# An order planner that counts two engines' SBUF operations longer in one passage

## The chip, the cores and the metric

The kernel runs on one core of a Trainium2 chip. The metric is the device time of one launch in microseconds (us). Three runs of the kernel before took 804.41, 806.04 and 806.45 us; their median is 806.04.

Six queues matter here: TensorE (PE, matmuls, results in PSUM banks), its weight loads (PEld), VectorE (DVE), ScalarE (ACT), GpSimd (POOL, which here works on SBUF only) and SyncE (SP), which issues DMAs. Each engine takes its instructions strictly in the order in which the program lists them, and waits at the first one whose inputs or destination are not ready.

## The reference

Three stages in a row. Attention over 32 memory slots, for 4 batches of 8 heads and 576 positions, gives a matrix of 2304 tokens by 512. A gated layer of 1536 hidden columns follows, and then a GELU layer of 2048:

```python
x = attn_out.transpose(0, 2, 1, 3).reshape(B * S, H * D)      # 2304 x 512
x = ((x @ moe_w_a) * (x @ moe_w_b)) @ moe_w_out               # 1536 hidden columns
h = x @ moe2_w_in                                             # 2048 hidden columns
out = (h * (1.0 / (1.0 + np.exp(-1.702 * h)))) @ moe2_w_out
```

## The kernel before

**Numbers.** Each float32 operand of a large product is split into a high part (a ScalarE copy that rounds, line 282) and a low part (the difference, line 276). A product then takes three matmul passes: high by high, low by high, high by low.

**First layer.** The 1536 hidden columns go in six groups `g` of 256. For each batch `b` and half `u` of 288 tokens, `gated(g, b, u)` runs 24 matmuls into four PSUM banks (line 800). `gated_out` then copies one bank (ScalarE, line 813), multiplies it by the other (VectorE, line 816) and splits the result into high and low. `proj(g, b, u)` runs 24 matmuls into four banks (line 833), and `proj_out` adds each bank to the sum in `acc` (VectorE, line 887).

**Second layer.** The product with `moe2_w_in` is done by `quad(g, p)`, for a group `g` of 256 hidden columns and a third `p` of the tokens (768 of them). It uses seven products of sums of half blocks in place of eight plain ones. Each product is a `step` of six matmuls of 384 columns (line 1066) into one bank. The first bank is copied (`kept`, ScalarE, line 1101), the other six are added to running sums (`added`, VectorE, line 1108, seven operations for a quad), and `gate` applies GELU and stores the block to DRAM (lines 1118 and 1120). The last stage, `proj2` (line 1174), reads these blocks back.

**The passage between the layers.** Before `quad(g, p)` can run, `combine_tokens(p, r)` (with `r` 0 and 1) must turn the sums in `acc` into seven operands, `yc[p]`, each split in two. By `seven` that is four additions or subtractions and seven splits for each `r`: 22 line-276 operations of 384 columns for one `p`, each on VectorE or on GpSimd, and 14 ScalarE copies. The operand with number 2 comes first, those with numbers 4 and 6 at the end of the chain. The products of a quad use the operands in the order 2, 4, 5, 3, 0, 6, 1. The passage begins when `room_early` is called, within the last group of the first layer. From there the main stream issues to TensorE, in this order: two `proj`, `gated(5,2,0)`, `gated(5,2,1)`, three `proj`, `gated(5,3,0)`, `gated(5,3,1)`, `quad(0,0)`, two `proj`, and then the quads (1,0), (0,1), (1,1), (0,2), (1,2), (2,0) and so on. The operands of `p` = 2 are only placed in `room_projected`, after the last `proj`.

**Buffers.** From the passage on, eight PSUM banks are shared by these steps (`bank_m`). A bank is free again when the last operation that reads it is done. The running sums of the quads (`hb_s`) and a buffer for decoding weights (`dm_s`) lie in the parts of `acc` that are free when `yc[0]` is done.

**Weights.** The float64 weights arrive as pairs of words and are decoded by `decode_piece`, five operations of 512 columns for a piece: ScalarE line 390, a maximum on VectorE or GpSimd (line 392), VectorE lines 396, 400 and 405. Then the raw buffer is free and SyncE can load the next piece into it (line 308).

**What sets the order.** The program is written by a planner, `Order`, when it is built. Each piece of work is a stream that asks for an engine with a ready time and a cost in ns (`dve(n)`, `act(n)`, `pool(n)`). `run` keeps a clock for each engine, and issues at each turn the request that can start first (in steps of 40 ns), among equals the one of lower priority number. PSUM work of `gated_out`, `proj_out`, `kept` and `added` has priority 0, the token operands have 5, 6 and 7. Where a request names two engines, `_plan` takes the one with the smaller sum of start, backlog, cost and `handicap`. The handicap of VectorE is 1000 ns (`W1`) from the end of attention on. The model's clocks decide the order on every engine; they don't wait for anything on the chip. As there is one main stream, the order of TensorE's matmuls in the passage is that of the list above, whatever the costs.

Of the kernel before, what the change touches and what calls it, by code (L numbers as in the profile page):

```python
# [12 lines left out]
ALU = mybir.AluOpType  # L13
# [6 lines left out]
PE, ACT, DVE, POOL = "PE", "ACT", "DVE", "POOL"  # L20
HOP, HOP_PE = 130.0, 200.0
W0 = 300.0
W1 = 1000.0
HOLD = {}
PR = 30
MBN = 8
# [17 lines left out]
def dve(n, fast=False):  # L44
    return 68 + n / (1.92 if fast else 0.96)


def act(n, psum=False):
    return (52 if psum else 94) + n / 1.2


def pool(n):
    return 150 + 2.1 * n


class Slots:


    def __init__(self, tiles=()):
        self.free = [[t, 0.0] for t in tiles]  # L60
# [11 lines left out]
class Order:  # L72
# [9 lines left out]
    def __init__(self):  # L82
        self.clock = {PE: 0.0, ACT: 0.0, DVE: 0.0, POOL: 0.0}
        self.dma, self.marks, self.streams, self.count = 2000.0, {}, [], 0

        self.handicap = {DVE: W0}

    def mark(self, t, *key):
        self.marks[key] = t
# [62 lines left out]
def tile_mem_attention_moe_moe2(  # L152
# [48 lines left out]
    od = Order()  # L201
# [70 lines left out]

    def combine(t, dst, in0, in1, op, n):

        t, e = yield {DVE: dve(n)} if op == ALU.max else {POOL: pool(n), DVE: dve(n)}, t
        (nc.gpsimd if e == POOL else nc.vector).tensor_tensor(out=dst, in0=in0, in1=in1, op=op)  # L276
        return t

    def hi_lo(t, hi, lo, src, n):

        t, _ = yield ACT, t, act(n)
        nc.scalar.activation(out=hi, in_=src, func=AF.Copy)  # L282
        return (yield from combine(t, lo, src, f32(hi), ALU.subtract, n))
# [10 lines left out]
    def raw_of(i):  # L294
        return raw_x if i == 2 * NHG - 1 else raw_s
# [82 lines left out]
    def decode_piece(t, i, name, part, n, m):  # L378

        plain = name[:2] == ("wab", 0)  # L380
        if plain:
            wt[name] = yield "slot", wab0_s
            t = max(t, wt[name][1])
        raw = loaded.pop(("raw", i))
        lw, hw = (raw[0][:, :, j].rearrange("p (n f) -> p n f", n=n) for j in range(2))
        mf = m[0].rearrange("p (n f) -> p n f", n=n)
        mu = mf.bitcast(U32)

        t, _ = yield ACT, t, act(512)
        nc.scalar.activation(out=mf, in_=hw.bitcast(F32), func=AF.Abs)  # L390
        t, e = yield {DVE: dve(512, True), POOL: 1456}, t
        (nc.vector if e == DVE else nc.gpsimd).tensor_scalar(  # L392
            out=mf, in0=mf, scalar1=2.0 ** -15, scalar2=None, op0=ALU.max
        )
        t, _ = yield DVE, t, dve(512, True)
        nc.vector.tensor_scalar(
            out=mu, in0=mu, scalar1=0x07FFFFFF, scalar2=3, op0=ALU.bitwise_and, op1=ALU.logical_shift_left
        )
        t, _ = yield DVE, t, dve(512)
        nc.vector.scalar_tensor_tensor(  # L400
            out=mu, in0=hw, scalar=0xC0000000, in1=mu, op0=ALU.bitwise_and, op1=ALU.bitwise_or
        )
        t, _ = yield DVE, t, dve(512)
        dst = wt[name][0].rearrange("p (n f) -> p n f", n=n) if plain else mf
        nc.vector.scalar_tensor_tensor(
            out=dst.bitcast(U32), in0=lw, scalar=29, in1=mu, op0=ALU.logical_shift_right, op1=ALU.bitwise_or
        )
        raw_of(i).release(raw, t)
        if plain:
            dm_s.release(m, t)  # L410
            od.mark(t, *name, part)
        elif name[0] == "in":
            decoded[name, part] = m
            od.mark(t, "decoded", name, part)
            if part == 1:
                od.spawn(PW if name[1] else PW0, combine_weights(name[1]))
        elif name[0] == "o2":
            c = name[1]
            t = max(t, (yield "mark", "room", *name))
            t = yield from hi_lo(t, wo2[c][:, HI], wo2[c][:, LO], m[0], DM)  # L420
            dm_s.release(m, t)
            od.mark(t, "wo2", c)
        else:
            if part == 0:
                wt[name] = yield "slot", slots_of[name[0]]
                od.mark(wt[name][1], "place", name)
            t = max(t, (yield "mark", "place", name))
            yield from split_weights(t, name, part, wt[name][0], m, dst, n)
# [7 lines left out]
    def split_weights(t, name, part, whole, m, src, n):  # L436
        view = {"o1": w_out_view, "wab": w_ab_view}[name[0]](whole)
        r = slice(part * n, (part + 1) * n)
        t = yield from hi_lo(t, view[:, HI, r, :], view[:, LO, r, :], src, 512)
        dm_s.release(m, t)  # L440
        od.mark(t, *name, part)
# [37 lines left out]
    def memory(n):  # L479
        b, g = divmod(n, NHG)  # L480
        t = yield "mark", "phi", n
        if n in HOLD:
            yield ("mark", *HOLD[n])
        ph = loaded.pop(("phi", n))
# [121 lines left out]
    def softmax(t, n, o, w, sT, place, left):  # L606
# [5 lines left out]
        sm1 = sm[0][:, 0:w // M, :]  # L612
        nc.vector.reduce_max(out=sm1[:, :, 0], in_=s3, axis=AX.X)
        t = yield from combine(t, s3, s3, sm1.to_broadcast(full), ALU.subtract, w)
        t, _ = yield ACT, t, act(w)
        nc.scalar.activation(out=s3, in_=s3, func=AF.Exp, scale=scale)
# [4 lines left out]
        t, _ = yield DVE, t, 125  # L621
        nc.vector.reciprocal(out=sm1, in_=sm1)
        t = yield from combine(t, s3, s3, sm1.to_broadcast(full), ALU.mult, w)
        sm_s.release(sm, t)
        if not place:
# [27 lines left out]
    def close_attention():  # L653
# [10 lines left out]
        pa.release()  # L664
        od.handicap[DVE] = W1
        nonlocal py, pz
# [233 lines left out]
    yc, win, wo2 = {}, {}, []  # L900
    win_s, hb_s, f_s, sb_s = Slots(), Slots(), Slots(), Slots()

    def views(m, n, count, o=0):
        return [m[:, o + i * n:o + (i + 1) * n] for i in range(count)]
# [4 lines left out]
    def parted(flat):  # L909

        assert len(flat) == 28
        return [[flat[4 * b + 2 * i:4 * b + 2 * i + 2] for i in range(2)] for b in range(7)]
# [4 lines left out]
    def spare():  # L917
        return next(x for x in (whl_a, big["whl_b"]) if x is not wt["o1", NG1 - 1][0])

    def place(p, operands):  # L920
        for b in operands:
            od.mark(now(), "place", p, b)
# [4 lines left out]

    def room_early():

        rest = views(big["y0"], YN, 9, 14 * WN)  # L930
        yc[0] = parted(views(big["wv"], YN, 16) + views(spare(), YN, 5) + rest[:7])
        yc[1] = parted(views(attn_m[0], YN, 12) + views(eff_m, YN, 4) + views(attn_m[1], YN, 12))
        used = wt["o1", NG1 - 1][0]
        yc[2] = parted(
            views(big["eff_b"], YN, 5) + views(used, YN, 5) + views(g1_m, YN, 9) + [None] * 6
            + views(eff_m, YN, 1, 4 * YN) + rest[7:]
        )
        place(0, range(7))
        od.spawn(9, room_kept())
        for p in range(NP):  # L940
            for r in range(2):
                od.spawn(PY + p, combine_tokens(p, r))

    def room_kept():

        n = KD * 2 * N2
        for r in range(2):
            yield "mark", "yc", 0, r
        give(hb_s, views(acc, N2, 6))
        give(dm_s, views(acc, DM, 1, 6 * N2))  # L950
        for r in range(2):
            yield "mark", "yc", 1, r
        give(hb_s, views(acc, N2, n // N2, n))
        for r in range(2):
            yield "mark", "yc", 2, r
        give(f_s, views(acc, FN, 1, 2 * n))

    def room_gated():

        place(1, (4, 5, 6))  # L960

    def room_projected():

        nonlocal p2
        p2.release()
        p2 = tc.alloc_tile_pool(name="p3", bufs=1, reuse_waits="tile")
        rest = p2.tile([P, 6 * YN], F32R, name="rest")
        for i, x in enumerate(views(rest, YN, 6), 19):
            yc[2][i // 4][i // 2 % 2][i % 2] = x
        place(2, range(7))  # L970
# [68 lines left out]
    def combine_weights(g):  # L1039
        m = [decoded[("in", g), k] for k in range(2)]  # L1040
        t = yield "mark", "decoded", ("in", g), 0
        t = max(t, (yield "mark", "decoded", ("in", g), 1))
        s = yield "slot", win_s
        win[g] = s
        (a11, a21), (a12, a22) = (
            [x[0].rearrange("p (r j f) -> p r j f", r=2, j=2)[:, :, j] for j in range(2)] for x in m
        )
        dst = [[x[:, HI], x[:, LO]] for x in s[0]]
        t = yield from seven(max(t, s[1]), PW if g else PW0, dst, a11, a12, a21, a22, True, 2 * P, ("win", g))
        for x in m:  # L1050
            retire_dm(x, t)
# [257 lines left out]
    with tc.manual_schedule():  # L1309
# [15 lines left out]
        for n in range(NU):  # L1325
            p = 10 + n if n >= NHG else 10 + PC * n
# [42 lines left out]
```

## Time and profile before

| what | value |
|---|---|
| median of three runs | 806.04 us |
| profiled execution, its own time | 806.26 us |
| its span (first to last instruction) | 804.4 us |
| mean granted TensorE clock | 0.995 |
| PE busy | 785.3 us (98%) |
| PEld busy | 704.9 us (88%) |
| DVE busy | 554.7 us (69%) |
| ACT busy | 387.5 us (48%) |
| POOL busy | 312.8 us (39%) |

The profiled execution took 806.26 us, 1.9 us more than its span, and 0.2 us more than the median. Busy times are sums over the span; an engine can be idle in the mean and full in one stretch. The granted clock is a share of full speed: 1.00 is 2.4 GHz and 0.50 is 1.2 GHz.

### The profile page before, as it was taken

The numbers are of one execution on the slowest core, as the hardware profiler recorded it, in microseconds if no ns is written. First come the engines' busy times: TensorE is split into PE (matmuls) and PEld (weight loads), VectorE is DVE, ScalarE is ACT, GpSimd is POOL, SyncE is SP. The second block draws the span as 40 slices with busy tenths as digits, with TensorE's granted clock in tenths as the row PEclk, the third lists the DMA queues.
The fourth block names the chain that finished last, engine by engine and source line by source line (L and its number), as shares of the span: only waits on it lengthen the run. The fifth ranks groups of instructions, "written<-read, shape, count | busy, mean of one in ns | idle before, by whom it ended". The sixth has DMA issues, their size and how long they took to land. (4 is left out here: it accounts for less than half of the span.)

```text
span 804.4 us, 13231 instructions
## 1 busy us (share of the span) xinstructions
PE 785.3 (98%) x4928; PEld 704.9 (88%) x4928; DVE 554.7 (69%) x988; ACT 387.5 (48%) x839; POOL 312.8 (39%) x304
## 2 busy tenths in 40 slices
PE   8989999999999999999998999999999999999997
PEld 7777788899989899999988999999998878888886
DVE  4888978989988876966999777776794852212100
ACT  4567767654654545544656454555554442222200
POOL 1224235555634435436697274444366420000000
PEclk9999999999999999999998999999999999999999
DMA  8866401233231210220001326754459556323001
GB/s 285 311 200 191 155 1 53 80 105 106 79 99 34 80 53 27 57 76 1 27 28 59 119 80 211 249 171 161 170 179 331 181 194 202 117 79 118 24 16 39
DMA packets 59327, 95.48 MB, mean 119 GB/s; under 512 B 5248, under 2 KB 42112, under 8 KB 59264
## 3 DMA queue, kind: packets, MB, share of 16 engines
q1 hardware_dynamic: 58432, 93.84, 35.8%
q10 hardware_dynamic: 832, 0.82, 0.3%
q8 instruction: 38, 0.62, 0.3%
q14 instruction: 25, 0.20, 0.1%
HBM read 71.04 MB, written 23.59 MB: 118 GB/s over the span
## 5 line engine op out<-in xcount | busy, mean ns | idle before, releaser
L1108 DVE TENSOR_TENSOR acc<-bank,acc 128x384 f32<-128x384 f32 x168 | 87.1, 550 | 33.2 <-PE bank L1066 16.4
L1118 ACT ACTIVATE acc<-acc 128x384 f32<-128x384 f32 x96 | 48.3, 522 | 59.9 <-DVE acc L1108 59.5
L276 POOL TENSOR_TENSOR y<-gr,y 128x288 fp32r<-128x288 f32 x43 | 37.6, 876 | 63.6 <-ACT y L282 63.0
L833 PE MATMUL bank<-g,whl_b 128*128 128x288 f32 x384 | 56.7, 307 | 4.2 <-DVE acc L1108 3.0
L833 PEld LDWEIGHTS bank<-g,whl_b 128*128 128x128 f32 x384 | 54.4, 197 | 5.9 <-DVE acc L1108 3.2
L816 DVE TENSOR_TENSOR gr<-bank,gr 128x288 f32<-128x288 f32 x96 | 43.1, 450 | 21.9 <-PE bank L800 11.2
L800 PE MATMUL bank<-attn,eff 128*128 128x288 f32 x384 | 55.1, 297 | 1.0 <-ACT eff L771 0.7
L276 DVE TENSOR_TENSOR attn<-acc,attn 128x1024 fp32r<-128x1024 f32 (+1 forms) x24 | 28.6, 1195 | 39.8 <-ACT attn L282 39.8
L800 PEld LDWEIGHTS bank<-attn,eff 128*128 128x128 f32 x384 | 52.2, 188 | 3.0 <-ACT eff L771 0.9
L392 POOL TENSOR_SCALAR dm<-dm 128x512 f32<-128x512 f32 x23 | 36.9, 1604 | 41.1 <-ACT dm L390 39.3
L1066 PE MATMUL bank<-attn,y 128*128 128x384 f32 x288 | 52.3, 335 | 0.0
L856 PE MATMUL bank<-y,whl_a 128*128 128x512 f32 (+1 forms) x240 | 51.5, 370 | 0.0
L813 ACT ACTIVATE gr<-bank 128x288 f32<-128x288 f32 x96 | 38.1, 400 | 26.8 <-PE bank L800 26.5
L1066 PEld LDWEIGHTS bank<-attn,y 128*128 128x128 f32 x288 | 50.1, 188 | 0.0
L856 PEld LDWEIGHTS bank<-y,whl_a 128*128 128x128 f32 x240 | 41.9, 188 | 8.0
L276 POOL TENSOR_TENSOR g<-gr,g 128x288 fp32r<-128x288 f32 x34 | 32.8, 969 | 37.8 <-ACT g L282 37.3
L1174 PE MATMUL bank<-wv,attn 128*128 128x512 f32 x180 | 43.1, 392 | 0.0
L282 ACT ACTIVATE y<-gr 128x288 fp32r<-128x288 f32 x48 | 21.4, 446 | 44.8 <-DVE gr L816 44.6
L800 PE MATMUL bank<-attn,eff_b 128*128 128x288 f32 x288 | 41.1, 297 | 1.4 <-DVE acc L887 1.1
L876 DVE TENSOR_TENSOR acc<-bank,acc 128x512 f32<-128x512 f32 (+1 forms) x72 | 38.0, 550 | 5.1 <-PE bank L856 4.4
L800 PEld LDWEIGHTS bank<-attn,eff_b 128*128 128x128 f32 x288 | 39.0, 188 | 2.6 <-DVE acc L887 1.8
L276 DVE TENSOR_TENSOR y<-acc,y 128x1024 fp32r<-128x1024 f32 (+1 forms) x13 | 15.8, 1216 | 36.6 <-ACT y L282 36.6
(262 smaller groups left out, 1961.9 us busy)
## 6 DMA issues: line engine op xcount, KB each, us to landing
g2d<-acc SPq DMA_DIRECT2D x96, 192.0 KB, 2.4
acc<-g2d SPq DMA_DIRECT2D x12, 1536.0 KB, 6.9
raw<-in_moe_w_out_dram SPq DMA_DIRECT2D x28, 512.0 KB, 4.2
raw<-in_moe_w_in_dram SPq DMA_DIRECT2D x16, 512.0 KB, 3.8
raw<-in_moe_w_a_dram SPq DMA_DIRECT2D x20, 256.0 KB, 2.9
raw<-in_moe_w_b_dram SPq DMA_DIRECT2D x20, 256.0 KB, 3.1
q<-in_q_dram SPq DMA_DIRECT2D x8, 576.0 KB, 6.3
out_dram<-dm SPq DMA_DIRECT2D x56, 64.0 KB, 1.7
```

The costliest lines, as they stand in the source:

```text
L276: (nc.gpsimd if e == POOL else nc.vector).tensor_tensor(out=dst, in0=in0, in1=in1, op=op)
L392: (nc.vector if e == DVE else nc.gpsimd).tensor_scalar(out=mf, in0=mf, scalar1=2.0 ** -15, scalar2=None, op0=ALU.max)
L800: nc.tensor.matmul(ps[0][:, :U], e[c][:, sw, i * CW + j * P:i * CW + (j + 1) * P], attn(b, mv, c, u * U, U), start=(n == 0), stop=(n == 3 ...
L813: nc.scalar.activation(out=gr[0], in_=pa_[0][:, :U], func=AF.Copy)
L816: nc.vector.tensor_tensor(out=gr[0], in0=pb[0][:, :U], in1=gr[0], op=ALU.mult)
L833: nc.tensor.matmul(ps[0][:, :U], w[:, sw, j, mb * P:(mb + 1) * P], g1[0][:, j, mv, :], start=(n == 0), stop=(n == 3 * G1 - 1),)
L856: nc.tensor.matmul(ps[0][:, :e - o], w[:, sw, j, mb * P:(mb + 1) * P], g1_all[mv][:, j, o:e], start=(n == 0), stop=(n == 3 * G1 - 1),)
L876: nc.vector.tensor_tensor(out=dst, in0=ps[0][:, a - o:z - o], in1=dst, op=ALU.add)
L1066: nc.tensor.matmul(ps[0][:, :N2], w[:, sw, r, :], y[mv][r], start=(n == 0), stop=(n == 5))
L1108: nc.vector.tensor_tensor(out=s[0], in0=ps[0][:, :N2], in1=x[0], op=ALU.add)
L1118: nc.scalar.activation(out=c[0], in_=c[0], func=AF.Gelu_apprx_sigmoid)
L1174: nc.tensor.matmul(ps[i, s][0], b[0][:, sw, c - h * KH, :], wo2[c][:, mv], start=(c == n == 0), stop=(c == 2 * KH - 1 and n == 2),)
```

## The change

The planner gets a flag, `shared`. It is set by `room_early`, and cleared by a new stream, `calm`, which waits until the operands of `p` = 1 and `p` = 2 are done in the model. While it is set:

- the additions and subtractions on SBUF (`combine`, line 276) are counted at 2.1 times their length on VectorE and 1.3 times on GpSimd;
- the last three operations of a decode are counted at 1.8 times;
- VectorE's handicap is 300 ns in place of 1000.

No operation is added or taken away; what the costs set is the order within each queue and, where two engines are allowed, which of them does the work.

```diff
+W3 = 300.0
     def __init__(self):
         self.handicap = {DVE: W0}
+        self.shared = False
     def combine(t, dst, in0, in1, op, n):
-        t, e = yield {DVE: dve(n)} if op == ALU.max else {POOL: pool(n), DVE: dve(n)}, t
+        both = {POOL: 1.3 * pool(n), DVE: 2.1 * dve(n)} if od.shared else {POOL: pool(n), DVE: dve(n)}
+        t, e = yield {DVE: dve(n)} if op == ALU.max else both, t
     def decode_piece(t, i, name, part, n, m):
+        slow = 1.8 if od.shared else 1.0
         t, e = yield {DVE: dve(512, True), POOL: 1456}, t
-        t, _ = yield DVE, t, dve(512, True)
+        t, _ = yield DVE, t, slow * dve(512, True)
-        t, _ = yield DVE, t, dve(512)
+        t, _ = yield DVE, t, slow * dve(512)
-        t, _ = yield DVE, t, dve(512)
+        t, _ = yield DVE, t, slow * dve(512)
     def room_early():
+        od.shared, od.handicap[DVE] = True, W3
+    def calm():
+        for p in (1, 2):
+            for r in range(2):
+                yield "mark", "yc", p, r
+        od.shared, od.handicap[DVE] = False, W1
     def room_projected():
+        od.spawn(9, calm())
```

## Rows read from the trace of the kernel before

**Rows 1.** The page's first part: busy time, share of the span, instructions.
```profile
PE 785.3 (98%) x4928; PEld 704.9 (88%) x4928; DVE 554.7 (69%) x988; ACT 387.5 (48%) x839; POOL 312.8 (39%) x304
```

**Rows 2.** Waits of PE: us in total, times, longest us.
```profile
PE bank L833 <- DVE acc L1108: 3.0, 1, 3.0
PE bank L800 <- DVE acc L887: 2.1, 3, 1.0
...
PE bank L1066 <- DVE acc L1108: 0.3, 1, 0.3
```

**Rows 3.** Busy us by stretch: PE, PEld, DVE, ACT, POOL; granted clock, DMA, GB/s.
```profile
140.00:160.00 20.00, 18.68 (x130) 17.50 (x129) 19.70 (x32) 12.12 (x26) 12.70 (x12) 1.00 0.27 80
388.00:448.00 60.00, 56.96 (x360) 55.53 (x360) 58.25 (x99) 32.13 (x71) 49.55 (x42) 0.94 0.14 45
419.75:424.65 4.90, 1.91 (x13) 1.64 (x12) 4.90 (x6) 2.79 (x6) 4.90 (x5) 0.93 0.00 0
424.65:432.34 7.69, 7.68 (x37) 7.57 (x38) 7.69 (x16) 4.18 (x7) 3.86 (x4) 0.60 0.28 102
```

**Rows 4.** Timeline of PE: start us, us, work, count, idle before it.
```profile
395.64 4.54 PE L833 MATMUL bank<-g,whl_b 128*128 128x288 f32 x33
...
405.19 4.98 PE L800 MATMUL bank<-attn,eff_b 128*128 128x288 f32 x34
...
411.85 1.21 PE L1066 MATMUL bank<-wv,y 128*128 128x384 f32 x6
...
419.75 1.91 PE L833 MATMUL bank<-g,whl_b 128*128 128x288 f32 x12
424.65 7.84 PE L833 MATMUL bank<-g,whl_b 128*128 128x288 f32 x36 [3.00 <-DVE acc L1108]
432.34 1.21 PE L1066 MATMUL bank<-wv,y 128*128 128x384 f32 x6
...
454.19 0.52 PE L1066 MATMUL bank<-whl_b,y 128*128 128x384 f32 x2
```

**Rows 5.** Timeline of ACT from 406 us.
```profile
410.13 0.67 ACT L390 ACTIVATE acc<-raw 128x512 f32<-128x512 f32 x1 [3.02 <-POOL y L276]
...
411.13 0.39 ACT L813 ACTIVATE gr<-bank 128x288 f32<-128x288 f32 x1
...
420.07 0.48 ACT L1101 ACTIVATE acc<-bank 128x384 f32<-128x384 f32 x1
```

**Rows 6.** Timeline of DVE, first and last of what the text uses.
```profile
410.84 0.43 DVE L392 TENSOR_SCALAR acc<-acc 128x512 f32<-128x512 f32 x1 [1.03 <-ACT acc L390]
...
419.25 0.44 DVE L816 TENSOR_TENSOR gr<-bank,gr 128x288 f32<-128x288 f32 x1
...
424.06 0.55 DVE L1108 TENSOR_TENSOR acc<-bank,acc 128x384 f32<-128x384 f32 x1
...
429.32 0.54 DVE L276 TENSOR_TENSOR attn<-acc,attn 128x384 fp32r<-128x384 f32 x1
...
430.25 3.00 DVE L887 TENSOR_TENSOR acc<-bank,acc 128x288 f32<-128x288 f32 x8
...
446.75 0.90 DVE L276 TENSOR_TENSOR y<-acc,eff 128x384 fp32r<-128x384 f32 x1
...
471.65 4.76 DVE L392 TENSOR_SCALAR dm<-dm 128x512 f32<-128x512 f32 x1
```

**Rows 7.** Timeline of POOL.
```profile
407.80 2.31 POOL L276 TENSOR_TENSOR y<-acc,y 128x384 fp32r<-128x384 f32 x2
...
432.61 1.01 POOL L276 TENSOR_TENSOR g<-acc,whl_b 128x384 fp32r<-128x384 f32 x1 [4.10 <-ACT whl_b L282]
```

**Rows 8.** Line 276 alone from 388 to 448 us: DVE, POOL, clock, DMA, GB/s.
```profile
388.00:448.00 60.00, 32.31 (x33) 48.27 (x41) 0.94 0.14 45
```

**Rows 9.** Waits of SP's queue, 390 to 450 us.
```profile
SPq L308 <- DVE acc L405: 19.4, 1, 19.4
```

## Prediction

> **What bounds the kernel now.** I read the page's busy shares first: PE is busy 785.3 of 804.4 us [rows 1], so all that a better order can give is some 19 us of idle PE and whatever its clock lost. The waits of PE come next. One wait stands out: a matmul of line 833 waits 3.0 us, once, for a line-1108 addition of VectorE; the next of its kind is 1.0 us at the longest [rows 2]. The busy times by stretch then say what it cost beyond itself. In the stretch behind it, 7.69 us long, the granted clock is 0.60 in the mean, and in the one before 0.93 [rows 3]. Of the two levels, 2.4 and 1.2 GHz, the lower held for 2 x (0.40 x 7.69) = 6.15 us, plus some 0.7 us of the idle time. Matmuls at half speed for 6.15 us lose 3.1 us.
>
> The timeline of PE gives the whole loss. The last three `proj` before the stall, 72 matmuls, take from 395.64 to 405.19 us, 9.55 us, so 48 take 6.37 us. Three quads without a wait take from 432.34 to 454.19, so one takes 7.28 us. From 411.85 to 432.34 PE does one quad and 48 `proj` matmuls: 20.49 us, where 7.28 + 6.37 = 13.65 would do [rows 4]. **Lost: 6.84 us**, of it 0.62 in the quad (411.85 to 419.75 is 7.90 us), 3.0 in the visible wait, the rest the clock and a small remainder.
>
> Why PE waited: eight banks are shared, and VectorE and ScalarE give them back late. `gated(5,3,1)` had left PE at 411.85, but its last line-816 product ran at 419.25. The first addition of quad(0,0) ran at 424.06, though PE had begun that quad at 411.85 [rows 4, 6]. Two things delayed them. From 388 to 448 us VectorE is busy 58.25 of 60 us [rows 3], and in its queue token splits and additions stand ahead of bank work. And ScalarE stood 3.02 us at line 390, whose buffer is free only when GpSimd's last write of `yc[0]` is done at 410.1 (407.80 + 2.31); behind it waited the line-813 copy that gives back a bank and starts the gated product [rows 5, 7].
>
> Both come from a clock in the planner that runs ahead of the chip. It counts a line-276 operation of 384 columns at 68 + 384/0.96 = 468 ns on VectorE and 150 + 2.1 x 384 = 956 ns on GpSimd, those of 288 at 368 and 755. For the mix from 388 to 448 us (30 and 3 on VectorE, 36 and 5 on GpSimd) that is a mean of 459 and 931 ns. Measured: 32.31/33 = 0.98 us and 48.27/41 = 1.18 us [rows 8]. The model is short by 2.13 and 1.26 times; so SBUF work that it thinks done in time for a bank's release is still running then.
>
> **The change, part by part.** It issues no instruction more or less. TensorE's order in the passage is that of the one main stream, and stays. Everything planned before `room_early` stays as well.
>
> *2.1 and 1.3.* A 384-column operation now counts 983 and 1243 ns, near the 0.98 and 1.18 measured. In the list the priority-0 work, ready when PE's step is done in the model, now falls ahead of SBUF operations which the model used to fit in before it. Lines 813 and 816, 1101 and 1108, and 887 move forward; the splits and additions of `yc[1]` move back; line 390 goes behind the line-813 copies, since `yc[0]` ends later in the model. What it can give back lies between nothing (the two engines are too full for any order) and the 6.84 us. I take the upper end less a remainder, since PE's own deadlines leave room, as follows.
>
> *What hides the work moved back.* At full pace PE would end quad(0,0) at 419.13, the last `proj` at 425.50, and start quad(0,1), the first user of `yc[1]`, at 432.78 and quad(0,2), the first of `yc[2]`, at 447.35 (432.78 plus two quads).
> - `yc[0]`: now done at 410.1 [rows 7]. Its last written operand feeds the sixth product of quad(0,0), five sevenths into it, at 417.1. Line-887 and line-816 work put ahead of it is some 3 us (the eight additions of 430.25 took 3.00 [rows 6]). Cover 7 us: no cost.
> - `yc[1]`: now done at 429.9 (429.32 + 0.54 [rows 6]). Put ahead of its last VectorE operations are at most seven additions at 0.55 us and the eight of 3.00, 6.9 us, less the 1.03 us in which VectorE stood idle for line 390 [rows 6]. It ends at 435.7 at worst; the last operand is due at 432.78 + 5.2 = 438.0. Cover 2.3 us: no cost; without it the stall comes again at quad(0,1).
> - `yc[2]`: now done at 447.65, 15.0 us after it could start at 432.61 [rows 6, 7]. It starts where the last `proj` is added up, so GpSimd's 4.10 us idle [rows 7] go, and 4.10/1.18 = 3.5 operations, at 15.0/22 = 0.68 us for each that the pair does, bring its end forward by 2.4 us. Against that, PE being a quad ahead wants up to six more additions by then, 3.3 us. It ends near 448.6; the second product of quad(0,2) is due at 448.4 (its operand is fourth of seven), the last chained one at 452.5. This is the thin cover. A remainder between 0 and 2 us; I take 1.0. A stall of that size costs itself alone: PE was idle 1.3 us in the stretch from 140 to 160, with the clock at 1.00 [rows 3].
>
> *Handicap 300.* With no backlog GpSimd is chosen by 1243 against 983 + 300, a 40 ns margin, where it was 956 against 1468. With both engines backed up the shares hardly move: an operation costs the model 1.26 times more on GpSimd than on VectorE, and VectorE has some six tenths of its time for them; before 2.04 times with VectorE held back 512 ns. I expect the 30 to 36 of now within four operations, and price four at nothing to half a microsecond either way, within the remainder.
>
> *1.8 for decodes.* One piece is decoded in the middle of the passage (410 us). It moves a few microseconds later. Its raw buffer is what SyncE waits for with the next load, 19.4 us today [rows 9]; the load and the stores queued behind it come later by as much. The next decode on VectorE is at 471.65 [rows 6], so some 55 us hide it. Nothing.
>
> *`calm`* puts the old costs back when `yc[2]` is planned. Behind 454 us PE waits once, 0.3 us, for line 1108 [rows 2], and weights, stores and loads hang on PE's own progress, so they shift with it. Between nothing and 0.5 us; I take nothing.
>
> **Sum.** 806.26 (the profiled execution; the median of the three runs is 0.2 lower) - 6.84 + 1.0 = **800.4 us**.
>
> **The rivals.**
>
> *A, the stall moves.* `yc[2]` is the bound: its second product waits, a stall of 3 us takes the clock down as it did here (3.1 us more), and 6.84 - 6.1 is all that is left: 805.5. If it is 2 us with no clock lost, 801.4, still the forecast. For it: VectorE full for 60 us. Against it: GpSimd's idle time and the 5 us between first and last due operand.
>
> *B, it doesn't do what it says.* VectorE is full whatever the order; additions pulled forward push splits that the same banks need (the gated split of line 276 feeds the very `proj` that stalled). The stall is 3 us again, 806.3. Against it: 3.02 us of ScalarE's wait and 1.03 of VectorE's [rows 5, 6] are pure order.
>
> *C, slower: VectorE locked out at line 392 or 396.* Today GpSimd happened to pause while line 392 ran at 410.84 (0.43 us, as did line 396), because ScalarE stood still; the row of 471.65 shows the same operation taking 4.76 us beside GpSimd operations in close succession [rows 6]. With ScalarE freed, GpSimd doesn't pause, and the handicap of 300 puts the maximum on VectorE rather than GpSimd (635 against 1456; it was 1335). Both operations locked out cost 2 x 4.33 = 8.7 us with bank work queued behind them. The order gains 3.0 + 1.0 us on the same queue, so it decides from some 4 us of lock-out on; at the full price the stall is 4.6 us longer and the time 806.26 + 4.6 = 810.9. Against it: over 60 us the passage has two such pieces at most, and a lock-out under 4 us only eats part of the gain.
>
> The Trainium skill ("SBUF — State Buffer", section "Who interferes with whom") has a rule that speaks for C: an operation in the two-port mode, which `tensor_scalar` can enter, and a GpSimd one exclude each other, and the later one blocks fully until the first is through. The trace agrees that it blocks, but 4.76 us is longer than one GpSimd operation of that stretch, so by the row the wait can last over several.
>
> **Chances.** Forecast 0.58 (799 to 802.5). A 0.12: half of it between 802 and 803.6, half near 805.5. B 0.14 (804 to 807.5). C 0.16 (808 to 811). A measurement of this kernel tells about 0.3%, 2.4 us, from no change, so faster means under 803.6, slower above 808.5. Faster: 0.58 + 0.06 + 0.02 of B and the edges = 0.66; slower 0.15; within it 0.19. The range from 798.8 to 807.5 leaves out C and little else. The forecast's own is 799 to 802.5.
>
> **What would show it.** Right: no wait of PE over 1.5 us between 405 and 460 us, clock 1.00 there; ScalarE's line 390 behind the last line 813; the first line 1108 before 418; the second quad starting near 425.5 and the last stage some 6 us sooner; VectorE's mean at line 276 still near 1 us. Wrong: a wait of 2 us or more at quad(0,1) or quad(0,2) with the clock at half (A); the 3 us wait where it was (B); a line 392 or 396 of over 2 us on VectorE in the passage (C). The forecast as a whole is wrong if the passage is clean and the time hasn't fallen: then later work, not PE's order, set the end.

## The result, and the profile after

The changed kernel takes 798.25 us (median), against 805.22 us of the kernel before in the same runs: a ratio of 0.9916, 95% interval 0.9900 to 0.9932. Measured again in more rounds (the first experiment below) it is 798.60 against 804.89 us, 0.9922 (0.9909 to 0.9935). That is 6.3 to 7.0 us faster. The forecast was 800.4 us; the time lies 0.55 us below the low end of the range, 798.8, and that of the second measurement 0.2 us below it.

One of the four executions behind the 798.25, the profiled one, took 1092.85 us at a mean granted clock of 0.66 (the other three have a median of 797.79, and the ratio goes by them), so the rows of after are those of the second measurement, whose profiled execution took 797.93 us. The change adds lines, so numbers move: the split 276 is 279, its ScalarE copy 282 is 285, the decode's 390, 392, 396, 400 and 405 are 394 to 409, 800, 813, 816, 833 and 887 are 804, 817, 820, 837 and 891, and 1066, 1101 and 1108 are 1079, 1114 and 1121.

Busy time on the page of after, to be read against [rows 1]:

```profile
PE 779.1 (98%) x4928; PEld 700.8 (88%) x4928; DVE 543.9 (68%) x984; ACT 387.5 (49%) x839; POOL 319.9 (40%) x308
```

VectorE is busy 10.8 us less, with four operations fewer, and GpSimd 7.1 us more, with four more. The same stretches as in [rows 3], by engine (PE, PEld, DVE, ACT, POOL, then granted clock), the second from the start of quad(0,0) to its end, the third the two `proj` behind it:

```profile
388.00:448.00 60.00, 60.00 (x401) 60.00 (x400) 55.85 (x106) 36.30 (x80) 53.43 (x46) 1.00 0.19 66
...
410.90:418.19 7.29, 7.29 (x45) 7.29 (x43) 6.46 (x13) 5.11 (x10) 5.69 (x6) 1.00 0.01 2
418.19:424.53 6.34, 6.34 (x49) 6.34 (x49) 5.81 (x11) 3.22 (x8) 6.34 (x7) 1.00 0.34 124
```

PE is busy without a gap and its clock is 1.00 throughout. The timeline of PE, to be read against [rows 4]:

```profile
404.55 6.51 PE L804 MATMUL bank<-attn,eff_b 128*128 128x288 f32 x48
410.90 1.20 PE L1079 MATMUL bank<-wv,y 128*128 128x384 f32 x6
...
418.19 6.50 PE L837 MATMUL bank<-g,whl_b 128*128 128x288 f32 x48
424.53 1.21 PE L1079 MATMUL bank<-wv,y 128*128 128x384 f32 x6
...
446.38 0.52 PE L1079 MATMUL bank<-whl_b,y 128*128 128x384 f32 x2
```

The 48 `proj` matmuls now run in one piece. From the start of quad(0,0) to that of quad(0,2) it is 446.38 - 410.90 = 35.48 us, where it was 454.19 - 411.85 = 42.34: 6.86 us less. ScalarE and VectorE in the same place, against [rows 5, 6]:

```profile
408.79 0.41 ACT L817 ACTIVATE gr<-bank 128x288 f32<-128x288 f32 x1
409.10 0.68 ACT L394 ACTIVATE acc<-raw 128x512 f32<-128x512 f32 x1
...
410.37 0.41 ACT L817 ACTIVATE gr<-bank 128x288 f32<-128x288 f32 x1 [0.27 <-PE bank L804]
...
412.74 0.47 ACT L1114 ACTIVATE acc<-bank 128x384 f32<-128x384 f32 x1
```

```profile
413.25 0.56 DVE L1121 TENSOR_TENSOR acc<-bank,acc 128x384 f32<-128x384 f32 x1
...
423.90 0.88 DVE L396 TENSOR_SCALAR acc<-acc 128x512 f32<-128x512 f32 x1
...
429.05 0.76 DVE L400 TENSOR_SCALAR acc<-acc 128x512 uint32<-128x512 uint32 x1
...
446.02 0.55 DVE L279 TENSOR_TENSOR y<-acc,eff 128x384 fp32r<-128x384 f32 x1
```

ScalarE doesn't wait at the decode any more (the line-394 row has no idle time behind it), and the first addition of quad(0,0) follows the quad's start by 2.35 us, where it was 12.21. I use this lag below as the measure of order; where PE itself is late, as in e7, it is longer for that reason too. The split line alone, against [rows 8]: DVE, POOL, clock.

```profile
388.00:448.00 60.00, 24.52 (x29) 52.81 (x45) 1.00 0.19 66
```

On balance four operations of this stretch went over to GpSimd, and one takes 0.85 us on VectorE in the mean, where it took 0.98.

### The profile page after: what moved, and what is told of

Its sections match the earlier page's. It is cut to its first block, busy times and chain, and to the rows that moved or that the text cites. A ratio compares the mean times of both kernels' runs of the same rounds, so it can differ in the third digit from the quotient of the medians.

```text
span 1091.1 us, 13229 instructions
## 1 busy us (share of the span) xinstructions
PE 1083.7 (99%) x4928; PEld 859.8 (79%) x4928; DVE 545.3 (50%) x984; ACT 398.0 (36%) x839; POOL 310.8 (28%) x308
## 4 chain that ended last, share of the span: by engine, by line
PE 99%; ACT 0%; issue 0%; DVE 0%; POOL 0%; POOLq 0%; DVEq 0%; ACTq 0%
PE bank L1187 26%; PE bank L1079 23%; PE bank L804 19%; PE bank L837 10%; PE bank L860 10%; PE bank L760 4%; PE bank L1219 2%; PE bank L548 1%; PE bank L592 1%; PE bank L467 1%; PE bank L729 1%; PE bank L507 0%; PE bank L528 0%; PE bank L510 0%; PE bank L570 0%; PE bank L532 0%
## 5 line engine op out<-in xcount | busy, mean ns | idle before, releaser
L804 PE MATMUL bank<-attn,eff 128*128 128x288 f32 x384 | 74.3, 364 | 0.0
L1079 PE MATMUL bank<-attn,y 128*128 128x384 f32 x288 | 73.2, 425 | 0.0
L804 PEld LDWEIGHTS bank<-attn,eff 128*128 128x128 f32 x384 | 70.5, 216 | 2.8 <-issue 1.8
L837 PE MATMUL bank<-g,whl_b 128*128 128x288 f32 x384 | 72.3, 363 | 0.0
L860 PE MATMUL bank<-y,whl_a 128*128 128x512 f32 (+1 forms) x240 | 72.2, 474 | 0.0
L837 PEld LDWEIGHTS bank<-g,whl_b 128*128 128x128 f32 x384 | 70.7, 215 | 1.0 <-issue 0.2
L1187 PE MATMUL bank<-wv,attn 128*128 128x512 f32 x180 | 60.7, 507 | 0.0
L1187 PEld LDWEIGHTS bank<-wv,attn 128*128 128x128 f32 x180 | 37.4, 208 | 21.3 <-issue 7.0
L804 PEld LDWEIGHTS bank<-attn,eff_b 128*128 128x128 f32 x288 | 53.1, 215 | 0.9 <-issue 0.2
L1079 PE MATMUL bank<-wv,y 128*128 128x384 f32 x192 | 51.3, 424 | 0.0
```

The costliest lines, as they stand in the source:

```text
L804: nc.tensor.matmul(ps[0][:, :U], e[c][:, sw, i * CW + j * P:i * CW + (j + 1) * P], attn(b, mv, c, u * U, U), start=(n == 0), stop=(n == 3 ...
L837: nc.tensor.matmul(ps[0][:, :U], w[:, sw, j, mb * P:(mb + 1) * P], g1[0][:, j, mv, :], start=(n == 0), stop=(n == 3 * G1 - 1),)
L860: nc.tensor.matmul(ps[0][:, :e - o], w[:, sw, j, mb * P:(mb + 1) * P], g1_all[mv][:, j, o:e], start=(n == 0), stop=(n == 3 * G1 - 1),)
L1079: nc.tensor.matmul(ps[0][:, :N2], w[:, sw, r, :], y[mv][r], start=(n == 0), stop=(n == 5))
L1187: nc.tensor.matmul(ps[i, s][0], b[0][:, sw, c - h * KH, :], wo2[c][:, mv], start=(c == n == 0), stop=(c == 2 * KH - 1 and n == 2),)
```

## The experiments

Two theories. **Theory 1, order**: the longer costs move the model's clocks on, so bank work is listed ahead of SBUF work. **Theory 2, split**: the new numbers hand more operations to GpSimd, and VectorE simply has less to do. **Theory 3** is a narrow rival: only ScalarE's wait at the decode mattered. Of the 66 token operations of 384 columns, 30 stand on VectorE before and 23 with the change; only 10 are the same ones, so 33 of the 66 changed their engine. "Lag" is the time from quad(0,0)'s start to its first addition, "passage" that from quad(0,0) to quad(0,2), both from the timelines.

| kernel | on VectorE | lag, us | passage, us | median, us | ratio to before (95%) |
|---|---|---|---|---|---|
| before | 30 | 12.21 | 42.34 | 804.89 | |
| e1 the change | 23 | 2.35 | 35.48 | 798.60 | 0.9922 (0.9909 to 0.9935) |
| e2 factors alone | 22 | 3.96 | 35.49 | 798.99 | 0.9925 (0.9913 to 0.9937) |
| e3 handicap alone | 33 | 8.64 | 37.26 | 803.92 | 0.9986 (0.9977 to 0.9994) |
| e4 late decode | 30 | 11.22 | 41.83 | 804.67 | 0.9997 (0.9988 to 1.0005) |
| e5 choose only | 32 | 10.35 | 39.55 | 805.21 | 1.0002 (0.9993 to 1.0011) |
| e6 book only | 25 | 2.35 | 35.49 | 798.48 | 0.9919 (0.9906 to 0.9933) |
| e7 counted twice | 32 | 7.84 | 43.03 | 811.25 | 1.0077 (1.0062 to 1.0093) |
| e8 old costs, handicap 1500 | 20 | 7.60 | 36.69 | 800.74 | 0.9946 (0.9934 to 0.9959) |
| e9 new costs, old engines | 30 | 2.67 | 35.49 | 798.23 | 0.9913 (0.9901 to 0.9924) |
| e10 old costs, new engines | 23 | 9.47 | 38.02 | 801.46 | 0.9954 (0.9942 to 0.9966) |
| e11 from attention on | 25 | 2.64 | 35.49 | 791.91 | 0.9834 (0.9822 to 0.9847) |
| e12 no decode factor | 23 | 2.36 | 35.49 | 798.04 | 0.9913 (0.9901 to 0.9925) |

(The median of before is that of e1 to e4's runs; it was 804.79 in the set of e5 to e8 and 804.99 in that of e9 to e12. e3 and e5 also lose time ahead of quad(0,0), which the passage column doesn't hold; they reach it at 415.55 and 414.04. e7 loses another 6.9 us in quad(0,2) itself, behind that column.)

**The parts of the change: e1, e2, e3, e12.**

> The change as it is, for an undisturbed profile. Theory 1 (order: bank work listed ahead of SBUF work): 798 us, no PE wait over 1 us between 405 and 460 us, granted clock 1.00 there, first line-1108 addition (now line 1121) before 418 us, VectorE's mean at the split line about 1.0 us. Theory 2 (split between engines): the same 798 us, but VectorE does clearly fewer or shorter 384-column operations, a mean under 0.9 us. Theory 3 (only ScalarE's block at the decode): the 3.02 us wait of the decode's first operation gone, VectorE as late as before.

> Only the factors 2.1 and 1.3; handicap stays 1000, decodes at their old length. Theory 1: most of the gain, 798 to 800 us, since the factors alone put bank work ahead. Theory 2: with the handicap at 1000 the split stays GpSimd's, 803 to 806 us. Theory 3: the planner lists the decode behind all line-813 copies here, so 798 to 800 us as well.

```diff
-W3 = 300.0
+W3 = 1000.0
-        slow = 1.8 if od.shared else 1.0
+        slow = 1.0
```

> Only the handicap 300; operations and decodes at their old length. Theory 1: the model's clock still runs ahead, so the stall at the second block of proj stays, 804 to 807 us. Theory 2: most of the gain, 798 to 800 us. Theory 3: the decode still stands ahead of the line-813 copies, 804 to 807 us.

```diff
-        both = {POOL: 1.3 * pool(n), DVE: 2.1 * dve(n)} if od.shared else {POOL: pool(n), DVE: dve(n)}
+        both = {POOL: pool(n), DVE: dve(n)}
-        slow = 1.8 if od.shared else 1.0
+        slow = 1.0
```

> The change without the 1.8 on decodes. The factors alone left a wait of 1.15 us at the second product of quad(0,2). If the handicap of 300 is what removes it, it is gone here as with the change, 798 to 799 us; if the decode's 1.8 removes it, it stays, some 799 to 800 us.

```diff
-        slow = 1.8 if od.shared else 1.0
+        slow = 1.0
```

e1 shows the signs of both theories: no wait of PE and the first addition before 418 us, as theory 1 had it, and a mean of 0.85 us on VectorE, under theory 2's 0.9. The two factors carry the gain; the handicap alone gives 0.1%. Neither run tells the theories apart, since the engines changed too: e2 has 22 operations on VectorE, where its theory 2 took the split to stay, and e3 has 33. In e3 the stall also didn't stay at the second block of `proj`, as expected; most of it moved ahead of quad(0,0), to a wait of 1.84 us in `gated(5,3,1)`, with 0.27 us left at `proj`.

The factors alone leave a wait that the change doesn't have. PE of e2, and VectorE of e2 behind it:

```profile
446.97 0.68 PE L1079 MATMUL bank<-g,y 128*128 128x384 f32 x3
448.79 0.79 PE L1079 MATMUL bank<-g,y 128*128 128x384 f32 x3 [1.15 <-DVE g L279]
```

```profile
446.76 1.98 DVE L279 TENSOR_TENSOR g<-acc,g 128x384 fp32r<-128x384 f32 x2
```

It is the second product of quad(0,2), which needs an operand of `yc[2]`. With the factors and the handicap, without the decode's 1.8 (e12), no wait of PE over 0.2 us stands between 380 and 480 us: from e2 to e12 only the handicap differs, so the 300 removes it. It isn't the only way: e6 below, with a handicap of 1000 and the engine chosen by the old costs (25 on VectorE), has no such wait either. It is 1.15 us in the trace; between the medians of e2 and e1 (0.39 us, overlapping intervals) it doesn't show.

**The narrow rival: e4.**

> The kernel before, with the decode's buffer in acc offered 15 us later in the model, so that the decode stands behind the line-813 copies; all costs as before. Theory 1: ScalarE's 3 us wait and VectorE's 1 us go, the rest of the lag stays: 801 to 804 us. Theory 2: 805 us. Theory 3: the whole gain, 798 to 800 us.

```diff
-        give(dm_s, views(acc, DM, 1, 6 * N2))
+        dm_s.free += [[x, now() + 15000.0] for x in views(acc, DM, 1, 6 * N2)]
```

The decode stands behind the line-813 copies here, and nothing is gained, less than theory 1 expected as well. The lag falls by 1 us only: token splits took the room. The stall came apart into five waits and the clock stayed up, so quad(0,0) and the 48 `proj` lost 18.11 - 13.65 = 4.5 us in place of 6.84; but the stretch from there to quad(0,2) took 23.72 us, not 21.85, with new waits at quad(0,1). PE of e4:

```profile
419.52 1.06 PE L833 MATMUL bank<-g,whl_b 128*128 128x288 f32 x6 [0.23 <-DVE gr L816]
420.79 1.06 PE L833 MATMUL bank<-g,whl_b 128*128 128x288 f32 x6 [0.21 <-ACT acc L1101]
423.37 1.06 PE L833 MATMUL bank<-g,whl_b 128*128 128x288 f32 x6 [1.53 <-DVE acc L1108]
424.64 1.06 PE L833 MATMUL bank<-g,whl_b 128*128 128x288 f32 x6 [0.20 <-DVE acc L1108]
426.38 3.44 PE L833 MATMUL bank<-g,whl_b 128*128 128x288 f32 x24 [0.69 <-DVE acc L1108]
...
447.48 1.31 PE L1066 MATMUL bank<-attn,y 128*128 128x384 f32 x6 [1.00 <-DVE acc L1108]
```

All engines of e4 in that stretch, the granted clock behind the five busy times:

```profile
411.00:430.00 19.00, 16.14 (x98) 14.56 (x97) 18.43 (x28) 10.97 (x24) 13.95 (x13) 1.00 0.12 42
```

Theory 3 falls.

**Order against split: e5, e6, e8, e9, e10.** In e5 and e6 a factor `k` (2.1 and 1.3) stands in one place of the planner only; the decode factor is off in both, the handicap 300 in e5 and 1000 in e6. The lines that mark the operations for `k` are left out of the two cuts, as are e5's `k` in the backlog and, further down, the names that e9 hands to `combine`.

> The new numbers (2.1, 1.3, handicap 300) only weigh in the choice of the engine; the model's clocks are still moved on by the old lengths. 32 of the 66 token operations of 384 columns then stand on VectorE (30 before, 23 with the change). Theory 1 (order): the model's clock runs ahead as before, the stall stays, 803 to 806 us. Theory 2 (split, fewer operations on VectorE): more of them on VectorE than before, so 805 to 807 us. Both far from 798.

```diff
-            if best is None or t + before + d + self.handicap.get(e, 0.0) < best[0]:
-                best = t + before + d + self.handicap.get(e, 0.0), (t, e, d)
+            if best is None or t + before + k * d + self.handicap.get(e, 0.0) < best[0]:
+                best = t + before + k * d + self.handicap.get(e, 0.0), (t, e, d)
```

> The reverse: the engine is chosen by the old numbers (handicap 1000), but the model's clocks are moved on by 2.1 and 1.3 times. 25 of the 66 on VectorE. Theory 1: the gain is there, 798 to 800 us. Theory 2: 25 is most of the way from 30 to 23, so 799 to 801 us too; it is the next two runs that tell them apart.

```diff
-                best = t + before + d + self.handicap.get(e, 0.0), (t, e, d)
+                best = t + before + d + self.handicap.get(e, 0.0), (t, e, k * d)
```

> Old lengths everywhere; only the handicap in the passage is 1500 in place of 1000. 20 of the 66 on VectorE, fewer than with the change. Theory 1: the model still counts GpSimd at 956 ns, so bank work is still listed late, part of the stall stays: 802 to 805 us. Theory 2: the gain is there, 797 to 800 us.

```diff
-W3 = 300.0
+W3 = 1500.0
-        both = {POOL: 1.3 * pool(n), DVE: 2.1 * dve(n)} if od.shared else {POOL: pool(n), DVE: dve(n)}
+        both = {POOL: pool(n), DVE: dve(n)}
-        slow = 1.8 if od.shared else 1.0
+        slow = 1.0
```

> The change, but each of the 66 token operations of 384 columns is held on the engine that it had before (30 on VectorE); the new costs set the order alone. Theory 1 (order): the gain is there, 798 to 801 us. Theory 2 (split): VectorE has as much to do as before, 804 to 807 us. If both count, 801 to 804 us.

```diff
+        if name and name[0] == "yc":
+            e = DVE if name in ON_DVE else POOL
+            both = {e: both[e]}
```

(`ON_DVE` lists the 30 operations that the kernel before has on VectorE.)

> The reverse: the kernel before with all its old costs, but each of the 66 is held on the engine that it has with the change (23 on VectorE). Theory 1: bank work is still listed late, 803 to 806 us. Theory 2: 798 to 800 us. If both count, 800 to 803 us.

The edit is the same in the kernel before, with the 23 of the change in `ON_DVE`.

Booking the longer time gives the whole gain (e6), using it in the choice alone gives none (e5). e9 is the cleanest run: all 66 operations where they were, 798.23 us, lag 2.67. PE and VectorE of e9, and its split line alone (DVE, POOL, clock):

```profile
411.62 1.20 PE L1115 MATMUL bank<-wv,y 128*128 128x384 f32 x6
...
418.91 6.50 PE L873 MATMUL bank<-g,whl_b 128*128 128x288 f32 x48
...
447.11 0.52 PE L1115 MATMUL bank<-whl_b,y 128*128 128x384 f32 x2
```

```profile
414.29 0.54 DVE L1157 TENSOR_TENSOR acc<-bank,acc 128x384 f32<-128x384 f32 x1
```

```profile
388.00:448.00 60.00, 27.08 (x34) 44.80 (x40) 1.00 0.13 47
```

Moving the 66 to other engines isn't needed. What e9 leaves free is small: the maximum of the decode in the passage went to GpSimd and one gated split to VectorE, and in the whole kernel the two engines have 988 and 304 operations, as before. But e8 and e10 show that theory 2 isn't empty, as theory 1 had it at 802 to 806: fewer operations on VectorE, with the old costs, give 3.5 to 4.1 us. PE and VectorE of e10:

```profile
422.03 4.25 PE L863 MATMUL bank<-g,whl_b 128*128 128x288 f32 x30 [1.03 <-DVE acc L1138]
427.22 1.06 PE L863 MATMUL bank<-g,whl_b 128*128 128x288 f32 x6 [0.94 <-DVE acc L1138]
```

```profile
420.33 1.18 DVE L435 SCALAR_TENSOR_TENSOR acc<-raw,acc 128x512 uint32<-128x512 uint32 x1
421.43 3.06 DVE L1138 TENSOR_TENSOR acc<-bank,acc 128x384 f32<-128x384 f32 x6
```

The additions are still listed behind splits and a decode, and six run in a row when their turn comes; but the queue ahead of them is shorter, so PE loses 2.5 us in place of 6.8, with the clock at 1.00. The planner lists anew when an operation changes its engine (before, splits stood between those six additions), so e8 and e10 don't show the split free of order, as e9 shows order nearly free of the split. The two effects don't add: either takes from the same 6.84 us, and order alone takes all of it.

**Too much of it: e7.**

> The change with twice its factors, 4.2 and 2.6. 32 of the 66 on VectorE, more than before, while all bank work stands far ahead of SBUF work. Theory 1: the stall at proj is gone as with the change; token operands come later, so up to 3 us are lost again at quad(0,1) or quad(0,2): 798 to 802 us. Theory 2: no gain, since VectorE has more of them than before: 805 us or more.

```diff
-{POOL: 1.3 * pool(n), DVE: 2.1 * dve(n)}
+{POOL: 2.6 * pool(n), DVE: 4.2 * dve(n)}
```

Slower than before. Theory 1 had nothing of that size; theory 2's "805 us or more" holds the time, but not by its reason, a VectorE with more to do. PE waits for no bank here; it waits for the operands themselves, at quad(0,0), quad(0,1) and quad(0,2):

```profile
416.12 0.79 PE L1079 MATMUL bank<-whl_a,y 128*128 128x384 f32 x3 [2.58 <-DVE whl_a L279]
417.40 0.79 PE L1079 MATMUL bank<-whl_a,y 128*128 128x384 f32 x3 [0.49 <-DVE whl_a L279]
440.69 0.61 PE L1079 MATMUL bank<-attn,y 128*128 128x384 f32 x2 [0.88 <-ACT attn L285]
441.79 1.73 PE L1079 MATMUL bank<-attn,y 128*128 128x384 f32 x7 [0.48 <-DVE attn L279]
458.85 0.83 PE L1079 MATMUL bank<-g,y 128*128 128x384 f32 x2 [2.64 <-ACT g L285]
460.58 1.33 PE L1079 MATMUL bank<-g,y 128*128 128x384 f32 x3 [0.90 <-DVE g L279]
```

Both engines idle meanwhile (VectorE is busy 46.83 and GpSimd 34.51 of 60 us). Between 395 and 465 us VectorE stands 5.8 us, in 15 pieces, at line-891 additions that wait for PE, where e1 has 0.5 us; the splits are listed behind them, and GpSimd in turn stands 13.6 us, in four pieces, for VectorE's operations. quad(0,2) alone costs 6.9 us: its first 38 matmuls take 13.51 us (455.01 to 468.52), in e1 6.62 (446.38 to 453.00). So not any delay of SBUF work gives the gain. The 7 us of cover that the prediction gave `yc[0]` are those of the sixth product's operand; the one that fails here is the second product's, due 4.2 us earlier.

**A faster version: e11.**

> The change, with the longer costs counted from the end of attention on (some 250 us earlier, handicap 1000 there) and not only in the passage. If the first layer's short waits of PE for line-887 additions and line-813 copies, 4.7 us between 120 and 200 us, have the same cause, 795 to 798 us. If they don't, 798 to 800 us; slower if splits of the gated product come late by it.

```diff
         od.handicap[DVE] = W1
+        od.shared = True
         nonlocal py, pz
```

791.91 us, 1.7% under the kernel before and 6.1 us under e12 of the same set, and 3.1 us below the low end of what I expected. PE, its weight loads and the other engines from 120 to 200 us, e1 first, then e11:

```profile
120.00:160.00 40.00, 37.30 (x249) 34.48 (x249) 37.53 (x58) 27.04 (x62) 23.37 (x21) 1.00 0.21 67
160.00:200.00 40.00, 37.97 (x270) 36.58 (x269) 36.04 (x79) 19.02 (x41) 21.48 (x18) 1.00 0.33 106
```

```profile
120.00:160.00 40.00, 39.70 (x280) 38.27 (x279) 38.02 (x65) 27.66 (x63) 23.98 (x22) 1.00 0.16 54
160.00:200.00 40.00, 40.00 (x290) 39.22 (x290) 34.74 (x67) 22.88 (x49) 25.16 (x22) 1.00 0.25 80
```

4.4 us of idle PE are back here, and PE runs 570 matmuls in these 80 us in place of 519; quad(0,0) starts at 403.84 in place of 410.90. The waits for additions are nearly gone, e1 first, then e11 (line 805 is line 804 of e1):

```profile
PE bank L804 <- DVE acc L891: 2.2, 3, 1.1
```

```profile
PE bank L805 <- DVE acc L892: 0.3, 1, 0.3
```

So the first layer gains by the longer costs too. Whether by order or by split isn't shown: the engines are free in e11, and over the whole kernel 12 more operations stand on GpSimd than in e1.

## Why the prediction was near and still missed

- **What bounds, and the 6.84 us.** Right. The passage gave back 6.86 us, and the clock stayed at 1.00. Of the 8.33 us between the two profiled executions, another 0.95 lie ahead of quad(0,0) and 0.52 behind the start of quad(0,2); the runs of one kernel lie that far apart.
- **The step that failed is the sum**, in two terms of much the same size: the base and the remainder. The forecast is 2.2 us above the 798.25: 1.04 by the base (806.26, where the same runs have 805.22), 1.0 by the remainder, 0.1 by the rest. Had only one of the two been off, the time would have come to 799.3, inside the range.
- **The remainder of 1.0 us** ("A remainder between 0 and 2 us; I take 1.0") measured zero: PE waits nowhere in the passage. `yc[2]` began at 426.90, 5.7 us earlier than before, and took 19.7 us where it took 15.0; I had moved its start by 4.1. It ended at 446.57 (446.02 + 0.55), not near 448.6, and the last split into `g`, which holds the second product's operand, was done at 442.20, some 5 us before that product:

```profile
440.83 1.37 DVE L279 TENSOR_TENSOR g<-acc,g 128x384 fp32r<-128x384 f32 x1
```

- **The handicap**, a step that I had priced at nothing to half a microsecond, is worth more with the factors: the wait that I had priced is real, 1.15 us at the product I named, but only in e2, where the handicap is 1000.
- **The base.** I subtracted from the profiled execution's 806.26 us, and said that the median stood 0.2 lower. In the runs of the result it is 805.22, and over the 23 runs of e1's set 804.89, 1.4 us under that execution. 805.22 - 6.84 is 798.38, where 798.25 was measured, and 804.89 - 6.84 is 798.05, where 798.60 was. How near each comes is in part luck: from one measurement to the other the two medians moved by 0.3 us each, in opposite directions.
- **Costs against measured means.** Right as far as tried: the measured 2.13 and 1.26 give the order that PE needs, and e7 shows what twice as much does. That they are the best isn't shown, as nothing between ran; with the change VectorE's operation takes 0.85 us, so the 983 ns are now too long by some 16%.
- **Shares hardly move, within four.** Wrong: from 30 to 23, seven on balance. By e9 the time didn't need it, by e10 it is worth 3.5 us with the old costs.
- **Line 390 behind all line-813 copies.** It stands before the last one, and no longer waits. The first addition ran at 413.25, ahead of the 418 named.
- **VectorE's mean near 1 us.** Wrong: 0.85, and 0.80 in e9 (27.08 us for 34), where the split is the old one.
- **Rival A** is e2 in small; in e7 its stall at quad(0,2) came in full, with others before it. **Rival B** falls with e9. **Rival C** fails on price: lines 392 and 396 stand on VectorE beside a running GpSimd, as it said, and took 0.88 and 0.76 us, together 0.8 us more than at 0.43 each, not 8.7. The rule of the Trainium skill's "SBUF — State Buffer" (section "Who interferes with whom") holds in that they get longer beside GpSimd; here by 0.45 and 0.33 us, less than one GpSimd operation of the stretch (1.17 us in the mean).

## What to carry to other kernels

Where a planner or a hand-made order lists work for engines that run in order, a cost that is too small on one engine lets low-priority work in ahead of what another engine waits for. Measure the mean of each group under the load of that very stretch, and book it: here about half of it on VectorE and three quarters on GpSimd lost 6.8 us, and twice as much 12.6 (811.25 against 798.60). The mean is itself a result of the order, so measure it again afterwards. And take the base of a prediction from as many runs as there are, not from the profiled one.

## What the runs showed of the hardware

**VectorE and GpSimd.** A 384-column operation with both inputs in SBUF takes VectorE 0.54 us where GpSimd is idle (429.32 us in [rows 6, 7]). Beside it the mean of line 276 is 0.98 us before and 0.80 in e9, for 33 and 34 operations of the same stretch, with all 66 token operations on the same engines. So how long the same work takes went by how the two queues were ordered against each other. Of the factor 2.13, 0.54 against the model's 468 ns is 1.15; the rest came with a busy GpSimd.

**The clock.** In e4, five waits of 0.20 to 1.53 us, 2.86 us in all between 419.3 and 426.4 us, left the granted clock at 1.00; behind the single wait of 3.00 us of the kernel before it was at 1.2 GHz for some 6.15 us, by its mean of 0.60 over 7.69 us [rows 3]. Behind a single wait of 1.84 us in e3, at 411.0 to 412.9 us, it fell too:

```profile
412.86 2.89 PE L804 MATMUL bank<-attn,eff_b 128*128 128x288 f32 x12 [1.84 <-DVE acc L891]
```

```profile
412.00:414.00 2.00, 1.14 (x6) 1.14 (x7) 2.00 (x5) 0.27 (x1) 1.33 (x1) 0.83 0.00 0
414.00:416.00 2.00, 2.00 (x10) 2.00 (x9) 2.00 (x6) 1.39 (x4) 0.00 (x0) 0.50 0.39 81
416.00:418.00 2.00, 2.00 (x11) 2.00 (x10) 2.00 (x4) 1.93 (x6) 1.21 (x1) 0.82 0.53 198
```

In e5 a wait of 1.56 us left it at 1.00, and 12 us later it was at 0.50 behind one of 1.74 us and a further 0.21:

```profile
412.35 1.85 PE L807 MATMUL bank<-attn,eff_b 128*128 128x288 f32 x12 [1.56 <-DVE acc L894]
...
424.99 1.06 PE L840 MATMUL bank<-g,whl_b 128*128 128x288 f32 x6 [1.74 <-DVE acc L1124]
```

```profile
426.00:428.00 2.00, 1.79 (x8) 1.74 (x8) 2.00 (x5) 0.84 (x3) 2.00 (x3) 0.50 0.00 0
```

So the price of a wait is not its length alone: the 3.00 us in one piece cost some 3.1 us more by the clock, the 2.86 us in parts nothing more by it. What tells the waits that bring the clock down from the others, these runs don't show.
